# Three edits at the start of a minimal-filtering convolution kernel: an earlier sum, one warm-up matmul, a moved transform job

## The chip, the cores and the metric

The kernel runs on one core of a Trainium2 chip. The metric is the time of one execution on the device in microseconds, lower is better. The core has five engines that run their own queues in order: PE (TensorE, matrix products into PSUM), DVE (VectorE), ACT (ScalarE), POOL (GpSimd) and SP (SyncE, which only issues DMAs here). PSUM has eight banks of 128 partitions x 512 fp32 values.

## The reference

A 1-d convolution with three taps over the sequence, then batch norm with given statistics, then silu. B = 2 sequences, S = 2048 positions, C = 1024 channels in and out, bf16.

```python
def reference(x, w, mean, var, g, b):
    xp = jnp.pad(x, ((0, 0), (P, P), (0, 0)))          # P = 1
    y = sum(jnp.einsum('bsc,cd->bsd', xp[:, k:k + S, :], w[k]) for k in range(K))   # K = 3
    inv_std = 1.0 / jnp.sqrt(var + 1e-5)
    y = (y - mean) * (g * inv_std) + b
    return _silu(y)
```

## The kernel before

**Method.** Six neighbouring outputs (R = 6) are computed from eight products (NJ = 8) instead of 18: eight inputs are transformed to the values at the points 0, 1, -1, 2, -2, 1/2, -1/2 and infinity, multiplied with the three taps transformed to the same points, and the eight products are combined to six outputs. A sequence has NB = 342 such blocks of six.

**Transform of x.** x is loaded in 17 windows of 128 positions (`load_x`, line 125, on the SP queue), each of which holds 21 blocks (the last one 6). Matmuls with the window as weights and the matrix rm as moving operand (`t_job`, line 322) give the transformed x with the channels in the partitions, in PSUM. A cast to bf16 takes them into `T_sb[bi]`: on ACT (line 333) or on DVE (line 335). A sequence needs 25 jobs: one for the window of 6 blocks, then three for each of eight pairs of windows, with 3, 3 and 2 of the eight channel tiles. A job of a pair has 6 (or 4) matmuls of 168 columns, fills two banks, and its cast has 1008 (or 672) values a partition. Which engine casts is decided while the program is written: a planner holds a clock for each engine (lines 108 to 116), adds costs for what it knows of, and each job goes to the engine on which its cast would end first (lines 324 to 331). What stands in the program is fixed.

**Transform of w.** For each of eight blocks of 128 output channels (dc), the taps are added up to the six inner points: even parts e0 = w0 + w2, e1 = 4 w2 + w0, e2 = 4 w0 + w2 (fp32), then u0 = e0 +- w1 (points +-1), u1 = e1 +- 2 w1 (points +-2) and u2 = e2 +- 2 w1 (points +-1/2), in bf16. Points 0 and infinity use w0 and w2 as they are. For block 0 GpSimd does all of it but the doubling of w1, which ACT does (`prepare_first`; line 213 writes f = 4 w0, line 216 g = 4 w2, line 218 the even parts, line 190 every u). The taps of block 0 are loaded among the windows of sequence 0, in the order w0, w2, w1 (W0_AT: behind the 6th, the 9th and the last window). The tiles for f, g and for doubled taps share one pool of two buffers in turn.

**Products.** A `Unit` is one block of channels for one sequence; the order is (dc, bi) = (0,0), (0,1), (1,0) and so on. Units use banks 0 to 3 and 4 to 7 in turn. A product (line 368) is eight matmuls of 342 columns into one bank, one for each channel tile; behind each matmul the function `between` is called. ACT copies banks (line 379, 381), DVE combines them (line 386), ACT applies silu (line 391). The later units spread the silu and the products of the outer rows over the next unit.

**Start.** PE first runs WARM matmuls of fp32 zeros (line 74), then the 25 jobs of sequence 0 (`ahead`; among them the transposes for rm0 and the parameters, which lead to the scales on GpSimd, lines 288 to 295). `prepare_first` writes its GpSimd instructions behind the scales, up to what needs no tap 1; the rest, which it returns as `left`, comes at the start of unit 0 (`run_first`). Unit 0 has eight products: points 0 and infinity, then 1, 2, -1, -2, 1/2, -1/2, into banks 3, 0, 3, 0, 3, 0, 2, 2. The last two share bank 2: ACT copies it after the seventh product, and the eighth adds on to it. Banks 1 and 4 to 7 are free for the jobs of sequence 1, which the object `between` (class `Between`) puts among the matmuls of unit 0: it counts matmuls (n), and the job with index q is written when n reaches at[q], for the first EARLY jobs. Their banks are (4,5), (6,7), (1,2) in turn; the jobs from EARLY on are written by `rest()`, behind the copy of the seventh product, in banks (6,7) and (4,5) in turn. Unit 1 starts with a product into bank 7 and reads the last windows of sequence 1.

Of the kernel before, what the change touches and what calls it, by code (L numbers as in the profile page):

```python
# [9 lines left out]
ALU = mybir.AluOpType  # L10
FP32 = mybir.dt.float32
# [4 lines left out]
P = 128  # L16
R = 6
NJ = 8
W0_AT = (5, 8, 16)
EARLY = 23  # L20
XBUFS = 12
T_FIRST = 21500.0
WARM = 2
WT = 21

@with_exitstack
def kernel(
# [10 lines left out]
    nc = tc.nc  # L38
    B, S, C = x.shape
    D = w.shape[2]  # L40
    CT, DC = C // P, D // P
# [9 lines left out]
    epool = ctx.enter_context(tc.tile_pool(name="epool", bufs=1))  # L51
# [20 lines left out]
    nc.vector.memset(zeros, 0.0)  # L72
    for _ in range(WARM):
        nc.tensor.matmul(ps[:, 7], lhsT=zeros[:, 0:P], rhs=zeros, start=True, stop=True)
# [73 lines left out]
    double, sums, act_work, dve_work = {}, {}, [], []  # L148
# [5 lines left out]
    def double_w(dc, eng):  # L154
        t = spool.tile([P, CT, P], BF16, name="w1x2")
        if eng is nc.scalar:
            nc.scalar.mul(t, raw[dc][:, 1], 2.0)
            busy("act", CT * P)
        else:
            eng.tensor_scalar(t, raw[dc][:, 1], 2.0, 0.0, op0=ALU.mult, op1=ALU.add)  # L160
        double[dc] = t
# [22 lines left out]
    def transform_w(dc, q, signs=(0, 1)):  # L184

        o = double[dc] if q else raw[dc][:, 1]
        if (dc, q) not in wts:
            wts[dc, q] = upool.tile([P, 2, CT, P], BF16, name=f"u{q}")
        for i in signs:
            nc.gpsimd.tensor_tensor(wts[dc, q][:, i], sums[dc, q], o, op=(ALU.add, ALU.subtract)[i])  # L190
# [17 lines left out]
    def prepare_first(dc):  # L208


        w0, w2 = raw[dc][:, 0], raw[dc][:, 2]
        g, f = (spool.tile([P, CT, P], BF16, name="w1x2") for _ in range(2))
        nc.gpsimd.tensor_scalar(f, w0, 4.0, 0.0, op0=ALU.mult, op1=ALU.add)
        for q, t, h in ((0, w0, w2), (1, g, w0)):
            if q:
                nc.gpsimd.tensor_scalar(g, w2, 4.0, 0.0, op0=ALU.mult, op1=ALU.add)
            sums[dc, q] = epool.tile([P, CT, P], FP32, name=f"e{q}")
            nc.gpsimd.tensor_tensor(sums[dc, q], t, h, op=ALU.add)

        def left():  # L220
            transform_w(dc, 0, (0,))
            double_w(dc, nc.scalar)
            transform_w(dc, 1, (0,))
            transform_w(dc, 0, (1,))
            transform_w(dc, 1, (1,))
            sums[dc, 2] = epool.tile([P, CT, P], FP32, name="e2")
            nc.gpsimd.tensor_tensor(sums[dc, 2], f, w2, op=ALU.add)
            transform_w(dc, 2)

        return left  # L230
# [66 lines left out]
    def t_jobs(bi):  # L297


        i = 0  # L300
        while i < NW:
            two = order[i:i + 2] if order[i] < NW - 1 else order[i:i + 1]
            i += len(two)
            n = LAST if two[0] == NW - 1 else WT
            wins = [
                (*xwin[bi, wi], rm if wi else rm0, min(P, S - (R * WT * wi - 1)) if wi else P - 1) for wi in two
            ]
            c0 = 0
            while c0 < CT:
                nct = min(512 // (NJ * n), CT - c0)  # L310
                yield wins, T_sb[bi][:, c0:c0 + nct, :, two[0] * WT:two[0] * WT + len(two) * n], n, c0, nct
                c0 += nct

    def t_job(job, bank):
        wins, dst, n, c0, nct = job
        nb, size = len(wins), nct * NJ * n
        clock["pe"] = max(clock["pe"], wins[-1][1], bank_free.get(bank, 0.0))
        src = ps[:, bank:bank + nb, 0:size]
        v = src.rearrange("p b (c j n) -> p b c j n", j=NJ, n=n)
        for q, (xw, _, mat, rows) in enumerate(wins):  # L320
            for c in range(nct):
                nc.tensor.matmul(  # L322
                    v[:, q, c], lhsT=xw[0:rows, (c0 + c) * P:(c0 + c + 1) * P], rhs=mat[0:rows, :, 0:n],
                    start=True, stop=True,
                )
        dst = dst.rearrange("p c j (b n) -> p (c j) b n", b=nb)
        src = src.rearrange("p b (q n) -> p q b n", n=n)
        clock["pe"] += nb * size / 2.3
        e = min(("act", "dve"), key=lambda k: ends(k, nb * size))
        busy(e, nb * size)  # L330
        bank_free[bank] = clock[e] + 100.0
        if e == "act":
            nc.scalar.copy(dst, src)  # L333
        else:
            nc.vector.tensor_copy(dst, src)  # L335
# [255 lines left out]
    def ahead(jobs, job_n):  # L591
        for job in jobs:
            t_job(job, job_n % 4 * 2)
            if job_n == 0:
                first_matrix()
            if job_n == 2:
                params()
            if job_n == 5:
                scales()
                left.append(prepare_first(0))  # L600
            job_n += 1
# [7 lines left out]
    class Between:  # L609
# [2 lines left out]
        n = done = 0  # L612
        jobs = list(t_jobs(1))
        at = [8, 12, 14, 16, 18, 20, 22] + [22 + (6 * CT - 22) * (q + 1) // (EARLY - 7) for q in range(EARLY - 7)]

        def do(self):
            t_job(self.jobs[self.done], (4, 6, 1)[self.done % 3] if self.done < EARLY else (6, 4)[(self.done - EARLY) % 2])
            self.done += 1

        def __call__(self):  # L620
            self.n += 1
            while self.done < EARLY and self.at[self.done] <= self.n:
                self.do()

        def rest(self):
# [34 lines left out]
    dc, bi = seq[-1]  # L660
# [45 lines left out]
```

## Time and profile before

| | us |
|---|---|
| three executions | 188.42, 188.44, 189.13 (median 188.44) |
| the profiled execution | 188.5 |
| its span, first to last instruction | 186.7 |
| first matmul of line 74 / of line 322 / of line 368 starts at | 1.45 / 5.10 / 19.31 |
| last jobs of sequence 1 start on PE at | 37.45 |
| GpSimd starts e2 of block 0 (line 227) at | 27.28 |
| mean granted clock of TensorE | 0.998 of full |

The groups that cost most (line, engine, operation, operands, count, busy time and mean ns of one, then the idle time before them and what ended most of it):

```profile
L368 PE MATMUL ps<-T_sb,u 128*128 128x342 bf16 (+2 forms) x816 | 120.1, 299 | 0.5 <-ACT yT L391 0.5
L190 POOL TENSOR_TENSOR u<-e,w1x 128x1024 bf16<-128x1024 f32 x32 | 69.4, 2194 | 3.9 <-DVE e L171 2.5
L335 DVE CAST T_sb<-ps 128x1008 bf16<-128x1008 f32 (+2 forms) x20 | 22.0, 1121 | 11.4 <-PE ps L322 11.2
L333 ACT CAST T_sb<-ps 128x1008 bf16<-128x1008 f32 (+2 forms) x30 | 24.9, 866 | 6.8 <-PE ps L322 6.6
L322 PE MATMUL ps<-rm,xw 128*128 128x168 bf16 (+2 forms) x272 | 24.8, 233 | 2.4 <-DMA xw<-in_x_dram 1.9
```

A matmul's mean is its time through a pipeline, not the distance to the next: successive matmuls start closer together than that. Idle time of an engine that others wait for is what counts.

### The profile page before, as it was taken

What the parts mean: (1) busy time and instruction counts of PE and PEld (TensorE: products, weight loads), DVE (VectorE), ACT (ScalarE), POOL (GpSimd) and SP (SyncE); (2) the same over time, 40 slices, a digit from 0 to 9 for tenths busy, and PEclk for the clock granted to TensorE, in tenths of its full rate; (3) what the DMA queues carried; (4) which work ended last, traced back from release to release, by engine and by line L of the source; (5) the groups of instructions that cost most, each with busy time, mean ns of one, the idle gap of its engine ahead of it and who ended that gap; (6) DMA issues with size and microseconds to landing.
All of it is one profiled execution on the core that took longest, in us unless ns stands there. A gap on an engine that the chain in (4) does not pass through costs nothing.

```text
span 186.7 us, 3721 instructions
## 1 busy us (share of the span) xinstructions
PE 177.0 (95%) x1402; PEld 125.0 (67%) x1402; DVE 154.9 (83%) x213; ACT 111.9 (60%) x182; POOL 146.1 (78%) x86
## 2 busy tenths in 40 slices
PE   6879999999999999999999999999999999999980
PEld 2658688776666666666666666666666666669980
DVE  5549667897979999999988998879988996769681
ACT  3789698689465565456545654565455555454790
POOL 3477999989998879999999999999999971021031
PEclk9999999999999999999999999999999999999999
DMA  5999999057607455798749667978596577979725
GB/s 168 315 351 334 381 388 232 4 151 193 123 4 142 102 109 130 196 187 198 150 109 210 115 136 201 202 178 167 115 199 117 123 79 163 181 140 167 162 62 112
DMA packets 86958, 31.72 MB, mean 170 GB/s; under 512 B 73542, under 2 KB 82778, under 8 KB 86940
## 3 DMA queue, kind: packets, MB, share of 16 engines
q1 hardware_dynamic: 85820, 31.24, 72.5%
q10 hardware_dynamic: 864, 0.21, 0.5%
q8 instruction: 11, 0.18, 0.4%
q0 software_dynamic: 256, 0.03, 0.2%
q14 instruction: 7, 0.06, 0.1%
HBM read 14.82 MB, written 8.39 MB: 124 GB/s over the span
## 4 chain that ended last, share of the span: by engine, by line
PE 83%; DMA 4%; DVE 4%; ACT 2%; SPq 2%; issue 1%; ACTq 0%; DVEq 0%
PE ps L368 77%; PE ps L322 5%; DVE T_sb L335 4%; DMA xw<-in_x_dram 3%; SPq L125 2%; DMA rows<-in_g_dram 1%; ACT yT L391 1%; ACT T_sb L333 1%; PE ps L534 1%; SPq L141 0%; ACTq L70 0%; DVEq L701 0%; ACT pc L379 0%; DVE sd L386 0%; DVE o L535 0%
## 5 line engine op out<-in xcount | busy, mean ns | idle before, releaser
L368 PE MATMUL ps<-T_sb,u 128*128 128x342 bf16 (+2 forms) x816 | 120.1, 299 | 0.5 <-ACT yT L391 0.5
L368 PEld LDWEIGHTS <-u 128*128 128x128 bf16 x816 | 76.7, 97 | 33.7 <-issue 0.7
L190 POOL TENSOR_TENSOR u<-e,w1x 128x1024 bf16<-128x1024 f32 x32 | 69.4, 2194 | 3.9 <-DVE e L171 2.5
L368 PE MATMUL ps<-T_sb,wch 128*128 128x342 bf16 (+2 forms) x272 | 43.0, 299 | 0.4 <-ACT T_sb L333 0.4
L391 ACT ACTIVATE yT<-ps,beta,scale 128x342 bf16<-128x342 f32 (+4 forms) x49 | 33.8, 721 | 11.9 <-PE ps L368 11.9
L190 POOL TENSOR_TENSOR u<-e,wch 128x1024 bf16<-128x1024 f32 x16 | 38.6, 2434 | 1.9 <-DMA wch<-in_w_dram 1.3
L386 DVE SCALAR_TENSOR_TENSOR t<-ps,sd 128x684 f32<-128x684 f32 (+2 forms) x51 | 39.1, 822 | 0.6
L368 PEld LDWEIGHTS <-wch 128*128 128x128 bf16 x272 | 25.6, 97 | 11.7 <-issue 0.7
L379 ACT COPY pc<-ps 128x342 f32<-128x342 f32 (+2 forms) x34 | 14.5, 427 | 30.1 <-PE ps L368 30.0
L335 DVE CAST T_sb<-ps 128x1008 bf16<-128x1008 f32 (+2 forms) x20 | 22.0, 1121 | 11.4 <-PE ps L322 11.2
L333 ACT CAST T_sb<-ps 128x1008 bf16<-128x1008 f32 (+2 forms) x30 | 24.9, 866 | 6.8 <-PE ps L322 6.6
L386 DVE SCALAR_TENSOR_TENSOR ps<-ps,t 128x684 f32<-128x684 f32 (+2 forms) x34 | 28.3, 832 | 0.6
L171 DVE SCALAR_TENSOR_TENSOR e<-wch 128x1024 f32<-128x1024 bf16 x12 | 27.2, 2263 | 0.0
L322 PE MATMUL ps<-rm,xw 128*128 128x168 bf16 (+2 forms) x272 | 24.8, 233 | 2.4 <-DMA xw<-in_x_dram 1.9
L322 PEld LDWEIGHTS <-xw 128*128 128x128 bf16 (+2 forms) x272 | 20.2, 97 | 8.3 <-DMA xw<-in_x_dram 3.0
L386 DVE SCALAR_TENSOR_TENSOR ps<-ps,pc 128x342 f32<-128x342 f32 (+2 forms) x34 | 16.8, 496 | 8.6 <-PE ps L368 7.5
L169 POOL TENSOR_TENSOR e<-wch 128x1024 f32<-128x1024 bf16 x7 | 16.9, 2409 | 0.0
L391 ACT ACTIVATE yT<-t,beta,scale 128x684 bf16<-128x684 f32 (+2 forms) x17 | 15.7, 926 | 0.0
L386 DVE SCALAR_TENSOR_TENSOR t<-ps,t 128x684 f32<-128x684 f32 (+2 forms) x17 | 13.9, 818 | 0.0
L576 POOL DMA_DIRECT2D out_dram<-o x2 | 1.4, 710 | 15.6 <-DMA o<-yT 15.6
L379 ACT COPY sd<-ps 128x342 f32<-128x342 f32 (+2 forms) x17 | 7.3, 429 | 9.7 <-PE ps L368 8.8
L381 ACT ACTIVATE pc<-ps 128x342 f32<-128x342 f32 (+2 forms) x17 | 7.5, 440 | 9.1 <-PE ps L368 6.8
(52 smaller groups left out, 61.3 us busy)
## 6 DMA issues: line engine op xcount, KB each, us to landing
xw<-in_x_dram SPq DMA_DIRECT2D x32, 256.0 KB
out_dram<-o SPq DMA_DIRECT2D x28, 192.0 KB
wch<-in_w_dram SPq DMA_DIRECT2D x9, 512.0 KB
out_dram<-o SPq DMA_DIRECT2D x14, 120.0 KB
wch<-in_w_dram SPq DMA_DIRECT2D x6, 256.0 KB
out_dram<-o SPq DMA_DIRECT2D x3, 128.0 KB
o<-yT SPq DMA_TRANSPOSE x15
out_dram<-o SPq DMA_DIRECT2D x12, 7.5 KB
```

The lines of the kernel that those rows point to most:

```text
L125: nc.sync.dma_start(out=xw[0:hi - lo, :], in_=x[bi, lo:hi, :])
L169: eng.tensor_tensor(e, w0, w2, op=ALU.add)
L171: eng.scalar_tensor_tensor(out=e, in0=f, scalar=4.0, in1=h, op0=ALU.mult, op1=ALU.add)
L190: nc.gpsimd.tensor_tensor(wts[dc, q][:, i], sums[dc, q], o, op=(ALU.add, ALU.subtract)[i])
L322: nc.tensor.matmul(v[:, q, c], lhsT=xw[0:rows, (c0 + c) * P:(c0 + c + 1) * P], rhs=mat[0:rows, :, 0:n], start=True, stop=True,)
L333: nc.scalar.copy(dst, src)
L335: nc.vector.tensor_copy(dst, src)
L368: nc.tensor.matmul(self.bank[q], lhsT=lhsT, rhs=T_sb[self.bi][:, ct, j, nsl], start=not add and ct == 0, stop=ct == CT - 1, skip_group_che ...
L379: nc.scalar.copy(dst, self.bank[q])
L381: nc.scalar.mul(dst, self.bank[q], by)
L386: nc.vector.scalar_tensor_tensor(out=out, in0=in0, scalar=scalar, in1=in1, op0=ALU.mult, op1=op1)
L391: nc.scalar.activation(self.yT[:, rows, self.lo:self.hi], src, ACT.Silu, bias=beta[:, dc:dc + 1], scale=scale[:, dc:dc + 1])
```

## The change

It has three parts.

- The even part e2 = 4 w0 + w2 of block 0 is written in `prepare_first` behind e1, ahead of the first instruction that needs tap 1, and no longer in `left` between u1 and u2. The instruction and its operands are the same.
- WARM is 1 instead of 2.
- EARLY is 22 instead of 23, and `at` gets one more entry, 6 CT + CT/2 = 52. Fifteen instead of sixteen jobs are spread from n = 22 to 48, the job with index 22 is written behind the fourth matmul of the seventh product, and the banks of the last two jobs change places (index 23: (4,5), index 24: (6,7)).

The list at for the indices from 7 on:

```
before  23 25 26 28 30 31 33 35 36 38 39 41 43 44 46 48
after   23 25 27 28 30 32 34 35 37 39 41 42 44 46 48 52
```

```diff
-EARLY = 23
+EARLY = 22
...
-WARM = 2
+WARM = 1
...
         nc.gpsimd.tensor_scalar(f, w0, 4.0, 0.0, op0=ALU.mult, op1=ALU.add)
-        for q, t, h in ((0, w0, w2), (1, g, w0)):
-            if q:
+        for q, t, h in ((0, w0, w2), (1, g, w0), (2, f, w2)):
+            if q == 1:
                 nc.gpsimd.tensor_scalar(g, w2, 4.0, 0.0, op0=ALU.mult, op1=ALU.add)
             sums[dc, q] = epool.tile([P, CT, P], FP32, name=f"e{q}")
             nc.gpsimd.tensor_tensor(sums[dc, q], t, h, op=ALU.add)
...
             transform_w(dc, 1, (1,))
-            sums[dc, 2] = epool.tile([P, CT, P], FP32, name="e2")
-            nc.gpsimd.tensor_tensor(sums[dc, 2], f, w2, op=ALU.add)
             transform_w(dc, 2)
...
         at = [8, 12, 14, 16, 18, 20, 22] + [22 + (6 * CT - 22) * (q + 1) // (EARLY - 7) for q in range(EARLY - 7)]
+        at += [6 * CT + CT // 2]
...
         def __call__(self):
             self.n += 1
-            while self.done < EARLY and self.at[self.done] <= self.n:
+            while self.done < len(self.at) and self.at[self.done] <= self.n:
                 self.do()
```

## The prediction

> **What bounds the kernel now.** I read the busy shares first, then stretches of the span, then what each engine did in time order in the first 40 us, where all three edits lie. The windows of the profile (length, busy time of each engine with its instructions, granted clock, DMA share, GB/s):
>
> ```profile
> PE 177.0 (95%) x1402; PEld 125.0 (67%) x1402; DVE 154.9 (83%) x213; ACT 111.9 (60%) x182; POOL 146.1 (78%) x86
> ...
> 9.60:13.50 3.90, 2.86 (x33) 2.24 (x33) 2.32 (x2) 3.42 (x5) 2.99 (x5) 1.00 1.11 342
> 13.50:19.30 5.80, 5.23 (x61) 4.47 (x62) 4.91 (x5) 5.19 (x8) 4.34 (x4) 1.00 1.10 340
> 19.30:30.00 10.70, 10.69 (x112) 8.56 (x112) 7.38 (x8) 7.99 (x12) 10.62 (x6) 1.00 1.07 372
> 30.00:38.00 8.00, 7.73 (x80) 6.15 (x78) 5.93 (x8) 5.98 (x9) 7.92 (x5) 1.00 0.32 62
> 38.00:51.00 13.00, 13.00 (x94) 8.74 (x92) 11.92 (x17) 9.89 (x15) 12.17 (x6) 1.00 0.66 162
> ```
>
> PE sets the end from 19.3 us on. Busy PE is not yet PE at full rate, so I compared the starts of successive matmuls in the single records with the closest spacing seen there: 72.5 ns at 168 columns, 145 ns at 342. By that PE loses 3.2 us from 5 to 13.5, 1.4 us to 19.3, 1.25 us to 38.2, 0.02 us to 52, 0.6 us to 60 and 0.1 us to 180. So an edit of the start can win no more than what is lost before 38 us; afterwards every 145 ns are a matmul. Where the first losses come from (start, length, engine, line, idle before):
>
> ```profile
> 1.45 3.71 PE L74 MATMUL ps<-zeros 128*128 128x512 f32 x4 [1.45 <-DVE dummy L76]
> 5.10 0.38 PE L322 MATMUL ps<-rm,xw 33*128 33x48 bf16 x8
> ...
> 9.59 2.58 PE L322 MATMUL ps<-rm,xw 128*128 128x168 bf16 x29 [0.96 <-DMA xw<-in_x_dram]
> 12.80 0.39 PE L322 MATMUL ps<-rm,xw 128*128 128x168 bf16 x3 [0.64 <-DMA xw<-in_x_dram]
> 13.49 5.37 PE L322 MATMUL ps<-rm,xw 128*128 128x168 bf16 x61 [0.30 <-DMA xw<-in_x_dram]
> 19.31 1.44 PE L368 MATMUL ps<-T_sb,wch 128*128 128x342 bf16 x8 [0.45 <-ACT T_sb L333]
> ```
>
> Up to 13.5 us PE waits for x; the windows put the DMA engines at 1.1 there. From 13.5 to 19.3 the casts L333 and L335 fill ACT (5.19 of 5.80) and DVE (4.91). The chain of waits shows the later losses, which are three waits for DVE:
>
> ```profile
> 30.86 1.22 DVE T_sb L335
> 32.09 0.04 issue
> 32.13 0.61 PE ps L322 x6
> ...
> 34.38 1.13 DVE T_sb L335
> 35.51 0.04 issue
> 35.56 0.61 PE ps L322 x6
> 36.17 0.02 issue
> 36.19 1.22 DVE T_sb L335
> 37.41 0.04 issue
> 37.45 0.89 PE ps L322 x10
> ```
>
> In the single records they cost 0.23, 0.23 and 0.30 us: jobs 17, 22 and 23 want banks (1; 6; 6) that the casts of jobs 14, 19 and 22 still read. Together 0.76 us.
>
> **One warm-up matmul less.** L74 shows four records for two matmuls, each some 1 us, starting 0.85 us apart; one matmul less frees 2 x 0.85 = 1.7 us of PE. The first real matmul (5.10) needs rm, whose last DVE instruction ends at 3.38 + 0.26 = 3.64. So it can start near 3.7, 1.4 us earlier. That is worth nothing at 13.49: PE stands 0.96 + 0.64 + 0.30 = 1.9 us waiting for x in between, and no load on the SP queue waits for PE that early (the 13th x load reuses the window read by 5.4 us and goes out at 9.11). Cost: 0; without this cover it would be a gain of up to 1.4 us.
>
> The clock is the other side of it. The windows print a granted clock of 1.00 from the span's start, and x12 matmuls of 168 columns from 5.54 take 1.03 us, the 72.5 ns spacing: full speed when the real work begins. What it is after half the warm-up no row shows. Bounds: nothing; or half speed, the 0.50 of the last 0.7 us of the span, thus 145 ns a matmul. At half speed 16 matmuls of a pair of windows take 2.3 us instead of 1.2; a pair of windows arrives each 1.4 us at the end (its last landings 13.45, 14.79, 16.17, 17.60 in the DMA records). Half speed up to 8.4 us vanishes in the 1.2 us in which PE then waits for x (8.4 to 9.6); up to 11.8 it nearly does in the other two waits. I take 0, since PE is nearly saturated by cold work from 3.7 us on.
> The Trainium skill ("TensorE: Matmul & The Clock Gate", Part 1: The HAM clock gate) says that the array starts at half clock and is released after about 3.4 us of sustained activity, and advises warming up for 4 us or more. Two warm-up matmuls give 3.6 us before the first real one, one gives 1.7; by the page the real matmuls then begin cold. The trace neither confirms nor denies it, its clock column being 1.00 throughout the start; the third rival is the time it could cost.
>
> **The sum of +-1/2.** These are the GpSimd rows:
>
> ```profile
> 15.49 2.12 POOL L218 TENSOR_TENSOR e<-w1x,wch 128x1024 f32<-128x1024 bf16 x1
> 18.91 2.13 POOL L190 TENSOR_TENSOR u<-e,wch 128x1024 bf16<-128x1024 f32 x1 [1.30 <-DMA wch<-in_w_dram]
> 21.00 2.12 POOL L190 TENSOR_TENSOR u<-e,w1x 128x1024 bf16<-128x1024 f32 x1
> ```
>
> e2 (2.12 us, at 27.28) moves into the gap of 1.30. It ends at 17.66 + 2.12 = 19.78, so u0+ starts 0.9 us later than 18.91 and ends near 21.9. Its reader, the third product, starts at 23.33: 1.4 us of cover. u1+ comes at 24.05 (needed 26.1), u0- at 26.1 (needed about 30). From u2 on GpSimd is 1.3 us earlier, 32.4 instead of 33.7 at its end, but PE takes u2 only at 36. Behind that the sums of block 1 wait anyway for its taps (32.2 and 33.3) and for ACT's times 4 (40.66). Sum: 0. Without the cover it costs up to 0.9 us. ACT's doubling (19.76) is untouched: its buffer is that of g, free at 17.6.
>
> **The moved job.** I followed the planner's own costs (lines 108 to 116, 324 to 331). Its choices for the jobs before the change match every cast in the ACT and DVE rows. With the new list jobs 9, 12, 13, 15, 16, 18, 19 come one matmul later, 17, 20, 21 two, 22 four; job 21 goes from ACT to DVE (its ends 36360 and 36003 instead of 36333 and 36429), job 22 from DVE to ACT (37154 against 41551, for DVE now has five combinations ahead of it). Each of the three waits goes: job 17 comes two matmuls (0.29 us) later with job 14 unmoved; job 22 comes 0.58 later with job 19 only 0.15; job 23 now has bank 4, last used by job 21, whose cast (0.86 on DVE) ends before it. Gain: 0.76.
>
> New waits, counted from a, the start of job 22 in the middle of product (2,5): its 6 matmuls take 0.44, ACT's cast starts at a+0.64 (0.27 after the last matmul's start, as at 38.09) and ends at a+1.64. Behind it on ACT stand the copy of bank 2, then the casts of 23 and 24. Product (2,5) ends at a+1.02, job 23 at a+1.45. Job 24 has bank 6, which job 22's cast frees at a+1.69: **0.25 us**. The copy runs 1.54 to 1.99, and product (2,6), which adds onto the bank it reads, waits to a+2.04: **0.06**. It ends at a+3.20. The cast of 23 starts at 1.89, that of 24 at 2.79 and ends at a+3.51. Unit 1 opens with bank 7, which job 24 now holds (before it was job 23's): **0.36**, to a+3.57. Against the free 0.76 stands 0.67: net **-0.1 us**. Check by places: job 22 started at 35.56; without two waits and four matmuls later a = 35.56 - 0.23 - 0.23 + 0.58 = 35.68, so unit 1 starts at 39.25 instead of 38.18 + 8 x 0.145 = 39.34. Bounds: all waits come back with ACT later still, +0.6; none of the new ones, -0.76.
>
> **Sum:** 0 + 0 - 0.1. The profiled run took 188.5 (span 186.7 and 1.8 around it); its median is 188.44, so **188.3 us**. The 0.6 us at 55.5 (unit 3 waits for ACT's silu) follows PE's own product at 53.5 and moves with it.
>
> **Rivals.** (1) The new waits don't arise, or half: the waits at 31 to 37 us simply go, -0.76: 187.7. For it: ACT is idle 1.08 us before the copy at 37.35. Against: the order on ACT, above. (2) The earlier start pulls the stage 13.5 to 19.3 forward, as its casts are the limit there: up to -1.4, 187.0. For it: ACT's 5.19 of 5.80. Against: PE's last wait for x ends only at 13.49, with DVE idle for 1.6 us before 14.35. (3) Slower: the clock stays at half past 13.5 us. Place: the last four pairs of windows. Two pairs cold are 32 x 72.5 ns = 2.3 us, less some 1.1 of PE's 1.4 us of waiting there: +1.2, 189.6; all four at half are 4.6 - 1.1 = +3.5. It decides only from 13.5 us; before, waiting for x covers it. (4) ACT's queue costs more than I gave (all new waits and none of the old ones gone): +0.6, 189.0. That the job doesn't move can't be; a total of zero is inside the forecast.
>
> **How the numbers follow.** Forecast 0.5 (own range 188.0 to 188.6), (1) 0.17, (2) 0.13, (3) 0.11, (4) 0.09. A change of 0.5%, 0.94 us, is about what measuring this kernel can tell from none. Faster by more: (2) and a quarter of (1), 0.17. Slower by more: (3) and part of (4), 0.15. Within: 0.68. The range reaches to (1) and (4) and part of the way to (2) and (3): 187.4 to 189.3.
>
> **What would show it.** L74 with two records and L322 starting near 3.7; PE still released by x near 13.5 and by ACT near 19.3; e2 before u0+ and no PE wait for POOL; no DVE wait of PE at 31 to 37, but waits for ACT (bank 6, bank 2, bank 7) at 37 to 39.5. Wrong if the first product starts more than 0.5 us off 19.31, the spacing of L322 is 145 ns past 13.5, or unit 1 starts before 38.8.

## The result and the profile after

The changed kernel is slower: 190.13 us against 188.54 (medians of 6 runs each), ratio 1.0077, 95% interval 1.0056 to 1.0098, which is some 1.45 us (the medians themselves lie 1.59 apart). Its profiled execution took 189.86 us with a span of 188.1, 1.4 more than before. (Lines behind the moved sum have moved up by two: L320 is the transform of x, before L322; L366 the products; L331 and L333 the casts on ACT and DVE.)

The start went as the prediction had it. PE in order of time in the changed kernel (start, length, engine, line, idle before):

```profile
1.45 2.08 PE L74 MATMUL ps<-zeros 128*128 128x512 f32 x2 [1.45 <-DVE dummy L76]
3.69 0.47 PE L320 MATMUL ps<-rm,xw 33*128 33x48 bf16 x8 [0.17 <-DVE rm L103]
...
4.29 1.43 PE L320 MATMUL ps<-rm,xw 128*128 128x168 bf16 x12
...
13.52 5.38 PE L320 MATMUL ps<-rm,xw 128*128 128x168 bf16 x61 [0.28 <-DMA xw<-in_x_dram]
19.35 1.42 PE L366 MATMUL ps<-T_sb,wch 128*128 128x342 bf16 x8 [0.45 <-ACT T_sb L331]
```

The first real matmul starts at 3.69 instead of 5.10, the first product at 19.35 instead of 19.31. The loss lies between 30 and 42 us, and there the sign "no DVE wait of PE at 31 to 37" fails: PE has one of about a microsecond. The windows of that stretch (length, then busy time and instructions of PE, PEld, DVE, ACT and POOL, clock, DMA share, GB/s), before:

```profile
30.00:42.00 12.00, 11.73 (x109) 8.89 (x107) 9.90 (x13) 9.49 (x14) 11.25 (x6) 1.00 0.42 100
```

and changed:

```profile
30.00:42.00 12.00, 10.29 (x98) 7.86 (x96) 9.86 (x13) 8.67 (x12) 8.70 (x6) 1.00 0.27 59
```

PE starts 11 matmuls less in the same 12 us, and no other engine is fuller. The chain of waits of the changed kernel in this place (start, length, what; "issue" is a short stretch with no wait that the profile names):

```profile
31.32 0.72 ACT T_sb L331
32.05 1.00 ACT T_sb L331
33.05 0.35 ACT sd L377
33.41 0.02 issue
33.43 0.51 DVE sd L384
33.94 1.13 DVE T_sb L333
35.07 0.04 issue
35.11 0.61 PE ps L320 x6
35.72 0.02 issue
35.74 1.01 ACT T_sb L331
36.75 0.04 issue
36.80 0.74 PE ps L366 x4
```

It is to be read backwards. The seventh product (36.80) goes into bank 2 and waits for ACT's cast at 35.74: that of job 20, which sits in banks (1,2). Jobs 14 and 17 have the same two banks. Job 20 itself (35.11) waited for bank 1, which DVE's cast of job 17 (33.94) freed. And that cast could have started about 1.1 us earlier, at 32.77 (0.27 us after the start of its job's last matmul): it stood on DVE behind the combination sd1 (33.43), which waited for ACT's copy into sd (33.05), which stood behind two casts on ACT (31.32 and 32.05). In the kernel before, the same cast stands ahead of sd1 on DVE, and the copy is done when sd1's turn comes:

```profile
32.76 1.21 DVE L335 CAST T_sb<-ps 128x1008 bf16<-128x1008 f32 x1 [0.69 <-PE ps L322]
33.88 0.50 DVE L386 SCALAR_TENSOR_TENSOR sd<-pc,ps 128x342 f32<-128x342 f32 x1
```

In the single records the waits of PE are 1.09 us (job 20), 0.67 (seventh product), 0.23 (job 24 for bank 6), 0.05 (the eighth product) and 0.37 (unit 1 for bank 7). The three waits of before, 0.76 together, are gone. From 19.3 to 42 us PE loses 2.82 us instead of 1.26. The list of waits between 19.4 and 42 us has, among the new ones, the one at the root (who waits for whom, total us, times, longest):

```profile
DVE sd L384 <- ACT sd L377: 1.4, 1, 1.4
```

### The profile page after: what moved, and what is told of

It is laid out like the page before. It is cut to its first block, busy times and chain, and to the rows that moved or that the text cites. A ratio compares the mean times of both kernels' runs of the same rounds, so it can differ in the third digit from the quotient of the medians.

```text
span 188.1 us, 3719 instructions
## 1 busy us (share of the span) xinstructions
PE 176.1 (94%) x1400; PEld 124.8 (66%) x1400; DVE 153.7 (82%) x213; ACT 112.0 (60%) x182; POOL 145.8 (77%) x86
## 4 chain that ended last, share of the span: by engine, by line
PE 82%; ACT 5%; DMA 4%; DVE 2%; SPq 2%; issue 2%; ACTq 0%; DVEq 0%
PE ps L366 77%; PE ps L320 5%; ACT T_sb L331 3%; DMA xw<-in_x_dram 3%; DVE T_sb L333 2%; SPq L125 2%; DMA rows<-in_g_dram 1%; ACT yT L389 1%; PE ps L532 1%; ACT pc L377 0%; SPq L141 0%; ACTq L70 0%; DVE sd L384 0%; DVEq L700 0%; ACT sd L377 0%
## 5 line engine op out<-in xcount | busy, mean ns | idle before, releaser
L366 PE MATMUL ps<-T_sb,u 128*128 128x342 bf16 (+2 forms) x816 | 120.2, 299 | 1.2 <-ACT T_sb L331 0.7
L366 PEld LDWEIGHTS <-u 128*128 128x128 bf16 x816 | 76.7, 97 | 34.7 <-issue 1.7
L366 PE MATMUL ps<-T_sb,wch 128*128 128x342 bf16 (+2 forms) x272 | 42.9, 299 | 0.5 <-ACT T_sb L331 0.5
L366 PEld LDWEIGHTS <-wch 128*128 128x128 bf16 x272 | 25.6, 97 | 11.7 <-issue 0.7
L331 ACT CAST T_sb<-ps 128x1008 bf16<-128x1008 f32 (+2 forms) x30 | 25.3, 876 | 8.8 <-PE ps L320 8.8
L333 DVE CAST T_sb<-ps 128x1008 bf16<-128x1008 f32 (+2 forms) x20 | 21.6, 1103 | 10.1 <-PE ps L320 9.9
L320 PE MATMUL ps<-rm,xw 128*128 128x168 bf16 (+2 forms) x272 | 25.5, 236 | 4.2 <-DMA xw<-in_x_dram 2.8
L320 PEld LDWEIGHTS <-xw 128*128 128x128 bf16 (+2 forms) x272 | 20.7, 99 | 10.2 <-DMA xw<-in_x_dram 5.6
L171 DVE SCALAR_TENSOR_TENSOR e<-wch 128x1024 f32<-128x1024 bf16 x12 | 25.8, 2148 | 0.0
L384 DVE SCALAR_TENSOR_TENSOR sd<-pc,ps 128x342 f32<-128x342 f32 (+2 forms) x17 | 8.2, 485 | 7.4 <-ACT sd L377 7.2
```

The source lines that it names most:

```text
L171: eng.scalar_tensor_tensor(out=e, in0=f, scalar=4.0, in1=h, op0=ALU.mult, op1=ALU.add)
L320: nc.tensor.matmul(v[:, q, c], lhsT=xw[0:rows, (c0 + c) * P:(c0 + c + 1) * P], rhs=mat[0:rows, :, 0:n], start=True, stop=True,)
L366: nc.tensor.matmul(self.bank[q], lhsT=lhsT, rhs=T_sb[self.bi][:, ct, j, nsl], start=not add and ct == 0, stop=ct == CT - 1, skip_group_che ...
L384: nc.vector.scalar_tensor_tensor(out=out, in0=in0, scalar=scalar, in1=in1, op0=ALU.mult, op1=op1)
```

## The experiments

Three theories. **Q** (queues): the whole loss is in the moved jobs, through the order on DVE and ACT and the bank that a job holds. **C** (clock): it comes from the missing warm-up. **S** (sum): from GpSimd's outputs being later by the moved sum. All ratios are against runs of before on the same chip, with the 95% interval. As the first product starts between 19.12 and 19.73 us in the profiled executions, I also give the time from it to unit 1's first product, which is what the moved jobs can change (before 20.03 us, changed 21.59, from the single records of one execution each).

| kernel | median us | ratio to before | first product to unit 1, us |
|---|---|---|---|
| third part alone | 190.57 | 1.0077 (1.0054 to 1.0100) | 21.72 |
| one warm-up matmul alone | 188.86 | 0.9998 (0.9981 to 1.0015) | 20.02 |
| earlier sum alone | 188.51 | 0.9989 (0.9973 to 1.0005) | 20.01 |
| changed, sd1 ahead of the copy | 189.22 | 1.0018 (1.0004 to 1.0032) | 20.52 |
| changed, job 17 at 40 | 189.11 | 1.0020 (1.0002 to 1.0039) | 20.69 |
| changed, jobs 17, 22 and two banks | 188.43 | 0.9982 (0.9959 to 1.0004) | 19.74 |
| earlier sum and four moves | 188.12 | 0.9973 (0.9953 to 0.9992) | 19.52 |
| earlier sum and a searched list | 187.84 | 0.9957 (0.9936 to 0.9977) | 19.51 |
| late tap | 190.65 | 1.0121 (1.0087 to 1.0155) | 20.09 |
| late tap, earlier sum | 188.68 | 1.0005 (0.9986 to 1.0024) | 20.12 |
| no warm-up | 188.80 | 1.0003 (0.9986 to 1.0020) | 20.02 |

### Each part alone

The first is before with the third part of the diff, the second with the second, the third with the first.

> Before with the third part alone (22 early jobs, one at the 52nd matmul). Theory Q (queues: job 17's cast now stands behind DVE's first combination sd1, which waits for ACT's copy of bank 3; job 20's cast then holds bank 2 when the seventh product wants it): all of the loss is here. PE waits of about 1.1, 0.7, 0.2 and 0.4 us between 33 and 41 us, unit 1 starts near 40.9 instead of 39.34, time 1.4 to 1.7 us over before. Rival C (the clock after half the warm-up): no change, within 0.3 us of before, since both warm-ups are there. Rival S (the earlier sum delays GpSimd's first outputs): no change.

> Before with one warm-up matmul alone. Theory Q: within 0.3 us of before; real matmuls start near 3.7 us at half speed (140 ns instead of 72.5) until about 5, and the first product still starts at 19.3. Rival C: 1 to 1.5 us slower.

> Before with the earlier sum alone. Theory Q: within 0.3 us of before; u0+ ends near 21.8 instead of 21.0, no PE wait for GpSimd. Rival S: PE waits for u, up to 0.9 us slower.

The third part alone gives the ratio of the whole change, 1.0077, and PE's waits at the same places: 1.09, 0.67, 0.23 and 0.37 us; the last matmul ahead of the first of them starts at 33.92, in the changed kernel at 33.88. The other two parts are not told from before. C and S fall, as causes of this loss.

### What makes job 17's cast late

In the changed kernel the two lines behind the product of point -1 change places:

```diff
             self.product(3, 2, True, between)
-            self.copy(3, dst=sd[:, 0])
             self.combine(sd[:, 1], pa, 2.0, b3, ALU.subtract)
+            self.copy(3, dst=sd[:, 0])
```

> The changed kernel with one pair of instructions of unit 0 exchanged: DVE's combination sd1 is written ahead of ACT's copy of bank 3, so that it doesn't wait for that copy. Theory Q: sd1 starts near 32.2 instead of 33.4, job 17's cast follows at once, and PE's wait of 1.09 us near 34 goes; the wait for bank 2 (0.7) and those of the last jobs (0.2, 0.4) stay: about 1.0 us faster than the changed kernel, 0.5 slower than before. If instead DVE's cast of job 17 is late for another reason (DVE too full), the wait stays and the time is that of the changed kernel.

DVE in order of time in this kernel:

```profile
31.05 1.21 DVE L333 CAST T_sb<-ps 128x1008 bf16<-128x1008 f32 x1 [0.45 <-PE ps L320]
32.43 0.51 DVE L384 SCALAR_TENSOR_TENSOR sd<-pc,ps 128x342 f32<-128x342 f32 x1 [0.17 <-PE ps L366]
33.01 3.40 DVE L333 CAST T_sb<-ps 128x1008 bf16<-128x1008 f32 x3
```

sd1 is now released by PE and starts a microsecond earlier, job 17's cast follows at 33.01, and PE's wait of 1.09 is gone; 0.67, 0.23 and 0.37 are left. The time falls by about 1.1 us against the changed kernel (the difference of the ratios, 0.0059). So sd1 does wait for the copy when it is written behind it, and this wait, handed on by DVE's queue, is the largest piece of the loss. Why it waits, no run separates: both instructions read bank 3, and both write the tile sd, in different halves.

The second way to the same end leaves the pair alone and moves job 17 by a single matmul; by an added argument each cast keeps the engine that it has in the changed kernel:

```diff
-at: ... 37 39 41 42 44 46 48 52
+at: ... 37 39 40 42 44 46 48 52
```

> The changed kernel with one number of the list changed: job 17 is written behind the 40th matmul instead of the 41st, so that its cast stands ahead of DVE's first combination sd1; all casts keep the engines that they have in the changed kernel. Theory Q: the wait of 1.09 us near 34 goes, the waits for bank 2 (0.67), bank 6 (0.23) and bank 7 (0.37) stay; about 1.0 us faster than the changed kernel, 0.5 slower than before. Rival D (the exchange of engines, job 21 on DVE and job 22 on ACT, is what costs): the 1.09 stays, time as changed.

```profile
33.20 1.21 DVE L333 CAST T_sb<-ps 128x1008 bf16<-128x1008 f32 x1 [0.69 <-PE ps L320]
34.32 0.50 DVE L384 SCALAR_TENSOR_TENSOR sd<-pc,ps 128x342 f32<-128x342 f32 x1
```

The cast now comes before sd1, and the 1.09 us go; 0.67, 0.23 and 0.37 stay. One matmul of 0.145 us in the place of a job was worth some 1.1 us. Rival D, that the exchange of engines costs it, falls for this wait: the engines are those of the changed kernel here. The next run has them too.

### The rest of the loss

```diff
-at: ... 37 39 41 42 44 46 48 52      banks of jobs 22, 23, 24: 6, 4, 6
+at: ... 37 39 40 42 44 46 48 48      banks of jobs 22, 23, 24: 6, 6, 4
```

> The same, and job 22 back at the 48th matmul, ahead of the seventh product, and the banks of the last two jobs as before ((6,7), then (4,5)); the engines still those of the changed kernel. Theory Q: the waits for bank 2 and bank 7 and that of job 24 go as well, one for bank 6 of about 0.4 (job 22 behind job 19's cast) and one of 0.1 come; unit 1 starts near 39.1, 1.9 us faster than the changed kernel, 0.2 faster than before. Rival D: still slower than before.

PE has one wait above 0.15 us left between 19 and 55 us, 0.39 us for bank 6. With job 22 ahead of the seventh product, bank 2 is free when that product comes; with job 24 in banks (4,5), unit 1 finds bank 7 free. The whole loss is gone with these moves, and the engines of the casts are still the exchanged ones. The 0.2 us by which it was to beat before can't be told from nothing (0.9959 to 1.0004).

### Two versions that beat both

The sum of rows that gives these waits (72.5 and 145 ns a matmul, a cast 0.27 us after its job's last matmul has started, 1.0 and 0.72 us on ACT, 1.21 and 0.86 on DVE, the copy and the combinations in their order) was then used to choose. The first version is before with the earlier sum and

```diff
-at: ... 33 35 36 38 39 41 43 44 46 48      (jobs 13 to 22)
+at: ... 33 34 36 38 39 41 43 44 46 46
-casts of jobs 19 and 20: DVE, ACT
+casts of jobs 19 and 20: ACT, DVE
```

> Before with the earlier sum and four moves, found by adding up the rows: job 14 at matmul 34 instead of 35, job 22 at 46 instead of 48, job 19's cast on ACT instead of DVE, job 20's on DVE instead of ACT. Theory Q: the waits at 31 to 37 us fall from 0.76 to about 0.2; unit 1 starts near 38.8; 0.5 us faster than before, plus up to 0.3 from the earlier sum. If the sum of the rows leaves something out, as my prediction's did, other waits come in their place and it is no faster.

Its windows row for the stretch shown above has PE without a gap:

```profile
30.00:42.00 12.00, 12.00 (x112) 9.23 (x110) 10.46 (x14) 9.97 (x15) 10.59 (x6) 1.00 0.45 111
```

The second has sd1 ahead of the copy, and for jobs 9 to 22 another list (25 25 27 30 32 32 34 37 37 39 39 42 43 46 47 from job 8 on) and engines (from job 8 on DVE casts 8, 9, 12, 14, 16, 19 and 21, ACT the others).

> Before with the earlier sum, sd1 ahead of ACT's copy of bank 3, and a list and engines for jobs 9 to 22 found by a search over the same sum of rows. Theory Q: PE waits below 0.15 us between 20 and 39 us, unit 1 starts near 38.7, 0.6 us faster than before, plus up to 0.3 from the earlier sum. It has less room against late casts than four_moves.

Both beat before and the changed kernel: 0.9973 and 0.9957, or 1.0 and 1.2% below the changed one. Which of the two is better is not settled: the intervals overlap, and the time between first product and unit 1 is the same to 0.01 us. How much of their gain is the jobs' (20.03 to 19.5, half a microsecond) and how much the sum's, the medians don't separate; the next pair shows what the sum is for. In the profiled execution of the second version PE still waits 0.26 and 0.22 us in units 1 and 2, in spite of the earlier sum. The chain of waits leads back through GpSimd to the first sum of block 1, which waited 1.30 us for its taps: the later one landed at 34.49 instead of 33.28. The earlier sum is no help against that.

### What the earlier sum is worth

In the profiled executions tap 1 of block 0 landed at 18.85 (before), 19.24 (changed), 20.20 (third part alone) and 20.39 us (one warm-up alone), with the same loads ahead of it. In the run with one warm-up alone PE had waits of 0.38 and 0.21 us in units 1 and 2 that before doesn't show. So I loaded the tap later, without the earlier sum and with it:

```diff
-W0_AT = (5, 8, 16)
+W0_AT = (5, 8)
...
-    for wi in order:
+    for i, wi in enumerate(order):
         load_x(1, wi)
+        if i == 2:
+            load_w(0, 1, 0)
```

> Before with tap 1 of block 0 loaded behind the third window of sequence 1 instead of ahead of the first, so that it lands some 1.5 us later, as it did by itself in two profiled runs. Theory P (the earlier sum is room for GpSimd against a late tap): GpSimd's whole row of outputs moves 1.5 us later, and as u2 of block 1 has about 0.5 us to spare, PE waits for it in units 1 and 2: 0.5 to 1.0 us slower than before. Rival: other work covers GpSimd anyway, no change.

> The same late tap with the earlier sum. Theory P: the sum fills the longer wait, GpSimd is no later than in before, and the time is within 0.2 us of before, 0.5 to 1.0 faster than the late tap without it. Rival: as slow as the late tap alone.

In the late tap alone GpSimd starts u0+ here:

```profile
21.10 2.13 POOL L190 TENSOR_TENSOR u<-e,wch 128x1024 bf16<-128x1024 f32 x1 [3.42 <-DMA wch<-in_w_dram]
```

which is 2.2 us later than in before, and PE stands still 25 us later:

```profile
46.44 5.96 PE L368 MATMUL ps<-T_sb,u 128*128 128x342 bf16 x40 [1.02 <-ACT pc L379]
53.63 1.34 PE L368 MATMUL ps<-T_sb,u 128*128 128x342 bf16 x8
```

The way there is seen in the run with one warm-up alone and a tap that was late by itself: ACT's multiplication of a tap by 4 waits until GpSimd has used the buffer, and the copy of a bank that PE waits for stands behind it on ACT:

```profile
44.38 1.06 ACT L239 ACTIVATE w1x<-wch 128x1024 bf16<-128x1024 bf16 x1 [0.57 <-POOL e L245]
45.35 0.43 ACT L379 COPY pc<-ps 128x342 f32<-128x342 f32 x1
```

With the earlier sum the same late tap costs nothing that can be told (ratio 1.0005, 0.9986 to 1.0024), without it the ratio is 1.0121: 2.0 us between the medians. Theory P, that the earlier sum gives GpSimd room against a late tap, holds for this tap. The cost was larger than expected (0.5 to 1.0). That the tap came 2.2 us later than before's and not 1.5 is part of the reason, I think; how much, no run shows.

### How far the waits for x cover the clock

> Before without any warm-up matmul. Theory Q: the clock is released later, perhaps only at 8 to 10 us, but PE still catches up in its waits for x before 13.5; first product at 19.3, time within 0.3 us of before. Rival C: without warm-up the first product starts late, 0.5 to 1.5 us slower.

```profile
4.29 2.01 PE L322 MATMUL ps<-rm,xw 128*128 128x168 bf16 x12
...
13.55 5.37 PE L322 MATMUL ps<-rm,xw 128*128 128x168 bf16 x61 [0.28 <-DMA xw<-in_x_dram]
19.37 0.85 PE L368 MATMUL ps<-T_sb,wch 128*128 128x342 bf16 x4 [0.45 <-ACT T_sb L333]
```

Twelve matmuls take 2.01 us instead of 1.03 in before: half speed. The record of the granted clock begins, with full speed, at 8.48 us here, at 4.97 in before, and the last pair of matmuls 140 ns apart starts at 8.31. The column of clocks prints 1.00 for the time ahead of the record too, where the matmuls are at half speed; so it says nothing of that time. But PE reaches the wait for x at 13.55 as ever, and the time is that of before. With one warm-up matmul it begins at 5.09 (changed) to 10.17 us (the version with jobs 17 and 22 moved), and in that one PE loses 1.40 us between 13.5 and 19.3, as before does (1.39). The cover that the prediction named reaches at least to 10 us.

## Why the prediction was wrong

- **Forecast 188.3, own range 188.0 to 188.6; measured 190.13**, above the whole range, which ended at 189.3. Slower by over 0.5% had a chance of 0.15.
- **The step that failed** is the count of waits under "The moved job": "Each of the three waits goes ... Gain: 0.76", against new waits of 0.67. The three waits did go, and the new ones that I counted came almost to the digit (0.25 for bank 6 was 0.23, 0.06 for the eighth product was 0.05, 0.36 for bank 7 was 0.37). What was left out is two more, 1.09 and 0.67 us. I checked for job 17 that its bank would be free when PE came, and not where its cast would then stand in DVE's queue: two matmuls later meant behind the 40th, thus behind sd1. And I checked the three banks of the rotation against each other, not bank 2 of job 20 against the seventh product, though it is that product's bank. So -0.76 + 0.67 became -0.76 + 0.65 + 1.76 = +1.65; measured at unit 1 +1.56.
- The planner didn't see it either: its model knows neither the order on an engine beyond one running clock nor who waits for sd1's copy. That I followed its arithmetic exactly (the engines of all casts came out as forecast) told where each cast goes, not when.
- **The bound from both sides** (-0.76 to +0.6) was made from the same incomplete list of waits; an omitted wait lies outside any such bound. Rival (4), ACT's queue, came nearest, since sd1's copy does stand behind two casts on ACT. But it had the old waits staying, which went, and none of the two that were left out, and its price, 0.6, is about a third of the loss.
- **One warm-up less: right**, a forecast of 0 and a measured ratio of 0.9998 (0.9981 to 1.0015), and for the reason given, the cover up to 13.5 us. One reading in it was wrong: "a granted clock of 1.00 from the span's start" is no reading of the clock, whose record begins at 4.97 us in before and at 5.09 in the changed kernel. The rows show what no row of before could: the real matmuls begin at half speed, 140 ns apart, and full speed comes at 5.09 us. The Trainium skill ("TensorE: Matmul & The Clock Gate", Part 1: The HAM clock gate) says too that the array starts at half clock. There the Trainium skill also says that the moment of release varies by some 500 ns from run to run, because its window runs free. Here, with a PE that is only partly busy, it varies by far more: 5.09 to 10.17 us with one and the same warm-up in five kernels. The advice of the Trainium skill to warm up for 4 us or more stands in the same page's section "Why this matters for your kernels" and is given there for measuring matmuls. Not following it cost no time here: the ratio with one warm-up matmul is 0.9998, with none 1.0003.
- **The earlier sum: right for the median, incomplete.** It cost nothing, with u0+ from 19.68 as forecast (19.8). But I put its gain at nothing because GpSimd was ahead of PE in one execution. The tap's landing moves by 2.0 us between executions, and block 1's outputs have only about half a microsecond to spare (in before the one that starts at 49.53 and takes 2.13 us is ready at 51.66, and PE takes it at 52.12).
- The 0.6 us at 55.5 moved with PE, as said: the matmul ahead of that wait starts at 57.06 instead of 55.47.

## What to carry to other kernels

When an instruction moves in a program with fixed queues, ask of it, on its own engine, which instruction it has passed and what that one waits for; the resource it writes is only half the question. A list of waits made for a forecast should go through each later user of every buffer in the stretch, not just through those that waited before; checking the list by replaying the rows of the known kernel is cheap, and here the corrected replay foresaw the ratios to before of five new versions to about 0.2 us. And an edit that only fills an idle gap can be worth something that one profile doesn't show, if the end of that gap is set by a transfer.

## What the runs showed that was not expected

A DMA of taps issued at the same place landed between 18.67 and 20.70 us in the eleven profiled executions that have the same loads ahead of it. In four of them it landed after 20 us, and in each of these one of its 16 parts came 1.2 to 1.5 us behind the other 15 (in the latest case 15 had landed by 19.20). The clock was granted in full between 5.09 and 10.17 us after the start with one warm-up matmul (five kernels), between 4.97 and 7.11 with two (seven), one execution of each kernel; so two warm-up matmuls don't always give full speed to the first real ones either. Neither is seen in the time of a kernel until its slack is used up: the half microsecond that block 1's outputs have to spare for the one, PE's waits for x for the other.
